# Retention attention into a gated MLP on one core: q and k in one tile, early values scaled on GpSimd, conversions and loads half a period earlier

## The chip, the core and the metric

The kernel runs on one core of a Trainium2 chip. The core has five engines that work side by side, each with its own queue of instructions that it takes in order: TensorE (PE) multiplies matrices, VectorE (DVE) and ScalarE (ACT) do elementwise work, GpSimd (POOL) does elementwise work and issues DMAs, and SyncE (SP) issues DMAs. The metric is the time of one execution on the device in microseconds (us), as the median of several runs. Smaller is better.

## What is computed

The first part is a recurrent attention (retention) with a decay for each head; the second is an MLP whose activation is h times cos(h). There are 4 batch elements, 8 heads, 768 positions and a head size of 64; the MLP has 3072 tokens, a model width of 512 and an inner width of 2048. All inputs and the output are float32.

```python
gamma = 1.0 - 2.0 ** (-5.0 - np.arange(H))
for t in range(S):
    state = gamma * state + outer(k[:, :, t], v[:, :, t])
    y[:, :, t] = (1 / sqrt(D)) * (q[:, :, t] @ state)
x = y.transpose(0, 2, 1, 3).reshape(B * S, H * D)
h = x @ w_in
out = (h * cos(h)) @ w_out
```

## The kernel before

**Chunks and pairs.** The sequence is cut into six chunks of 128 positions. One step of the attention handles one chunk of two batch elements, called a pair `p`; there are twelve pairs, six for batch elements 0 and 1 and then six for 2 and 3. The index `b` in 0, 1 names the batch element within a pair. The decay is separated into a factor on q that shrinks with the position (`gq`) and a factor on v that grows with it (`gk`); then the product of q and k within a chunk needs only a mask of zeros and ones, and the state that passes from chunk to chunk needs no decay.

**The steps of one pair.** `load` (line 110) brings float32 tiles of q, k and v (256 KB each) into SBUF. `conv_q`, `conv_k` and `conv_v` (lines 169 to 184) turn them into bfloat16: q times `gq` into `qs`, k copied into `ks`, v times `gk` into `vs`. There are three buffers of each, used in turn. The transposes of q and k into `qkt` are made by TensorE for pairs 0 to 3 (`stage_t`, line 191: eight transposes into one PSUM bank, then one copy of the bank by DVE or ACT) and by two DMA transposes on SP for pairs 4 to 11 (`stage_t_dma`, line 204: one for all of q, one for all of k). `stage_a` (line 217) multiplies k by q into two PSUM banks, `stage_m` (line 231) multiplies these by the mask into `am` on DVE, and `stage_y` (line 238) multiplies `am` by the values, adds the part that comes from the state `stb`, copies the result into `xt` on ACT, and updates the state in PSUM (`st_ps`), which it then copies into `stb`.

**The MLP.** A group `g` is two pairs, thus 512 tokens. `unit_f` (line 283) and `pair_f` (line 291, for the tokens of one pair) multiply `xt` by a part of `w_in`; `act` (line 274) makes the cosine on ACT and the product on DVE into `gt`. `unit_o` (line 307) multiplies `gt` by `w_out`, copies the bank on ACT, and stores it from SP.

**The order.** It is written out by hand (lines 341 to 480): each engine gets its instructions in the order in which the program lists them, and waits only where data or a buffer requires it. PSUM banks are taken from a list and given back to its end (class `Banks`). `warm(n)` (line 332) puts n matmuls of zeros into TensorE's queue. At the start pair 0 is handled separately: q is only cast, the decay and the mask are multiplied in as one factor `decay` that ACT makes with eight exponentials, and the values are cast without decay into `vu`; `conv_v(0)` on GpSimd is only for the state. GpSimd's queue at the start is: five loads of pairs 0 and 1 and more, `w_in` part 0, `conv_v(0)`, `w_in` part 1, `conv_v(1)`, `w_in` parts 2 and 3, the parts of `w_out` and the loads of pairs 2 and 3. In the steady part, `ahead(p + 1)` (line 435) converts a pair at the start of the half period before its use, `stage_t_dma(p + 1)` follows one unit later, and `later(p)` (line 441) does `stage_y(p)` and loads pair p + 3.

Of the kernel before, what the change touches and what calls it, by code (L numbers as in the profile page):

```python
# [10 lines left out]
FP32 = mybir.dt.float32  # L11
BF16 = mybir.dt.bfloat16
# [18 lines left out]
def kernel(  # L31
# [9 lines left out]
    nc = tc.nc  # L41
# [22 lines left out]
    def sb(shape, dt, name):  # L64
        return const.tile(shape, dt, name=name)
# [20 lines left out]
    qs = [sb([128, 2, H, D], BF16, f"qs{i}") for i in range(NB)]  # L86
    ks = [sb([128, 2, H, D], BF16, f"ks{i}") for i in range(NB)]
# [13 lines left out]
    rel = sb([128, 2, 128], FP32, "rel")  # L101
    decay = sb([128, H, 128], FP32, "decay")
    vu = sb([128, 2, H, D], BF16, "vu")
# [25 lines left out]
    def w_in_t(i, f):  # L129
# [6 lines left out]
    nc.gpsimd.iota(rel[:, 0], pattern=[[1, 128]], base=0, channel_multiplier=-1,  # L136
                   allow_small_or_imprecise_dtypes=True)
    nc.gpsimd.iota(pos, pattern=[[C, NC]], base=1, channel_multiplier=1,
                   allow_small_or_imprecise_dtypes=True)
    load(nc.gpsimd, 0, ("v0", "v1"))  # L140
    load(nc.gpsimd, 1, ("k0", "k1", "q1", "v0", "v1"))
# [3 lines left out]
    for h in range(H):  # L145
        nc.vector.memset(lgv[:, h : h + 1], lg[h])
    nc.vector.tensor_scalar(out=ident, in0=rel[:, 0], scalar1=0.0, scalar2=None,
                            op0=ALU.is_equal)
    nc.vector.tensor_scalar(out=rel[:, 1], in0=rel[:, 0], scalar1=0.0, scalar2=1.0e6,
                            op0=ALU.is_lt, op1=ALU.mult)  # L150
    nc.vector.tensor_tensor(out=rel[:, 1], in0=rel[:, 1], in1=rel[:, 0], op=ALU.add)
    nc.vector.tensor_scalar(out=mask, in0=rel[:, 0], scalar1=0.0, scalar2=None,
                            op0=ALU.is_ge)
    for h in range(H):
        nc.scalar.activation(out=decay[:, h], in_=rel[:, 1], func=AF.Exp, bias=lnsc,
                             scale=float(lg[h]))
    nc.vector.tensor_tensor(out=lgp, in0=pos.unsqueeze(2).to_broadcast([128, NC, H]),
                            in1=lgv.unsqueeze(1).to_broadcast([128, NC, H]), op=ALU.mult)
    nc.scalar.activation(out=gq, in_=lgp, func=AF.Exp, bias=lnsc)
    nc.scalar.activation(out=gk, in_=lgp, func=AF.Exp, scale=-1.0)  # L160
    nc.scalar.activation(out=cosb[0][:, :8], in_=lgp[:, 0, :], func=AF.Sin, scale=0.0)
    for t in stb:
        nc.vector.memset(t, 0.0)


    def bc(g, c):
        return g[:, c, :].unsqueeze(2).to_broadcast([128, H, D])

    def conv_q(p, eng):
        for b in range(2):  # L170
            eng.tensor_tensor(out=qs[p % NB][:, b], in0=qf[SLOT[p]][b],  # L171
                              in1=bc(gq, p % NC), op=ALU.mult)

    def conv_v(p, eng):
        for b in range(2):
            eng.tensor_tensor(out=vs[p % NB][:, b], in0=vf[SLOT[p]][b],  # L176
                              in1=bc(gk, p % NC), op=ALU.mult)

    def conv_k(p, on_act):
        for b in range(2):  # L180
            if on_act:
                nc.scalar.copy(out=ks[p % NB][:, b], in_=kf[SLOT[p]][b])  # L182
            else:
                nc.vector.tensor_copy(out=ks[p % NB][:, b], in_=kf[SLOT[p]][b])
# [6 lines left out]
    def stage_t(p, b, on_act):  # L191
        n = p % NB
        bank = banks.take()
        tr = bank.bitcast(BF16).rearrange("p (w a t) -> p w a t", w=2, a=HP)
        for w, src in enumerate((qs[n], ks[n])):
            for a in range(HP):
                nc.tensor.transpose(tr[:, w, a, :], src[:, b, 2 * a : 2 * a + 2, :], ident)  # L197
        if on_act:
            nc.scalar.copy(out=qkt[n][:, :, b], in_=tr)
        else:  # L200
            copy_bits(qkt[n][:, :, b], tr)
        banks.give(bank)

    def stage_t_dma(p):
        n = p % NB
        for w, src in enumerate((qs[n], ks[n])):
            nc.sync.dma_start_transpose(
                out=qkt[n][:, w].rearrange("p b a t -> p (b a) t"),
                in_=src.rearrange("p b h d -> p (b h d)"))

    def qt(n, b, a):
        return qkt[n][:, 0, b, a, :]

    def kt(n, b, a):
        return qkt[n][:, 1, b, a, :]
# [13 lines left out]
    decay_j = decay.rearrange("p (a j) t -> p j a t", j=2)  # L229

    def stage_m(p, item, parts=(0, 1)):
        b, bk, ap = item
        for j in parts:
            by = decay_j[:, j] if p == 0 else mask.unsqueeze(1).to_broadcast([128, HP, 128])
            nc.vector.tensor_tensor(out=am[p % 2][b][j], in0=ap[j], in1=by, op=ALU.mult)  # L235
            banks.give(bk[j])

    def stage_y(p, copy_st=nc.vector.tensor_copy):
        c = p % NC
        n = p % NB  # L240
        for b in range(2):
            bank = banks.take()
            yp = bank.rearrange("p (a t) -> p a t", a=HP)
            for a in range(HP):
                if c > 0:
                    for j in range(2):
                        nc.tensor.matmul(  # L247
                            yp[ts(j, 64), a, :], lhsT=stb[p % 2][:, b, a, ts(j, 64)],
                            rhs=qt(n, b, a), start=True, stop=False,
                            skip_group_check=True)  # L250
                for j in range(2):
                    nc.tensor.matmul(  # L252
                        yp[ts(j, 64), a, :], lhsT=(vu if p == 0 else vs[n])[:, b, 2 * a + j, :],
                        rhs=am[p % 2][b][j][:, a, :], start=(c == 0), stop=True,
                        skip_group_check=True)
            nc.scalar.copy(out=xt[(p // 2) % 2][:, :, ts(2 * (p % 2) + b, C)], in_=yp)  # L256
            banks.give(bank)
        if c == NC - 1:
            return
        for b in range(2):  # L260
            for a in range(HP):
                for j in range(2):
                    h = 2 * a + j
                    nc.tensor.matmul(  # L264
                        st_ps[ts(j, 64), b, a, :], lhsT=ks[n][:, b, h, :],
                        rhs=vs[n][:, b, h, :], start=(c == 0 and b == 0 and a == 0),
                        stop=True, skip_group_check=True)
        for j in range(2):
            copy_st(out=stb[(p + 1) % 2][ts(j, 64), :, :, ts(j, 64)], in_=st_ps[ts(j, 64)])  # L269

# [69 lines left out]

    load_w_in(0)
    conv_v(0, nc.gpsimd)
    load_w_in(1)
    conv_v(1, nc.gpsimd)
    load_w_in(2)
    load_w_in(3)
# [6 lines left out]

    warm(10)
    nc.vector.tensor_copy(out=qs[0][:, 0], in_=qf[0][0])
    for b in range(2):
        nc.vector.tensor_copy(out=ks[0][:, b], in_=kf[0][b])
    stage_t(0, 0, False)
    nc.vector.tensor_copy(out=qs[0][:, 1], in_=qf[0][1])  # L359
    for b in range(2):  # L360
        nc.scalar.copy(out=vu[:, b], in_=vf[0][b])
    a00 = stage_a(0, 0)
    stage_m(0, a00, (0,))
    stage_t(0, 1, False)
    stage_m(0, a00, (1,))
    warm(1)
    stage_m(0, stage_a(0, 1))
    conv_k(1, True)
    conv_q(1, nc.vector)
    warm(2)  # L370
    stage_y(0, nc.scalar.copy)
    stage_t(1, 0, False)
    stage_t(1, 1, True)
    warm(2)
    attend(1)
    banks.give(spare)
    pair_f(0, 0, (0,))
    stage_y(1, nc.scalar.copy)
    pair_f(0, 0, (1,))
    pair_f(1, 0)  # L380
# [5 lines left out]
    for part in range(3):  # L386
        for j in range(4):
            unit_o(0, j, part)
            if part == 2 and j == 0:
                stage_t(2, 0, False)  # L390
                stage_t(2, 1, False)
                conv_v(2, nc.vector)
            elif part == 2 and j == 1:
                stage_m(2, stage_a(2, 0))
            elif part == 2 and j == 3:
                stage_m(2, stage_a(2, 1))
# [12 lines left out]
    stage_t(3, 0, False)  # L409
    stage_t(3, 1, False)  # L410
# [16 lines left out]
    stage_t_dma(5)  # L427
    pair_f(3, 1)
# [3 lines left out]
    conv_v(6, nc.gpsimd)  # L432
    pair_f(3, 3)

    def ahead(p):
        if p < NP:
            conv_q(p, nc.gpsimd)
            conv_k(p, True)
            conv_v(p, nc.gpsimd)

    def later(p):
        stage_y(p)
        if p + 3 < NP:
            load(nc.sync, p + 3, ("q0", "q1", "v0"))
            load(nc.gpsimd, p + 3, ("k0", "k1", "v1"))
# [6 lines left out]
    stage_t_dma(6)  # L452
# [6 lines left out]
    for g in range(2, NG + 1):  # L459
        for s in range(16):  # L460
# [8 lines left out]
            if p < NP:  # L469
                if r == 0:  # L470
                    ahead(p + 1)
                elif r == 1:
                    todo = [stage_a(p, b) for b in range(2)]
                    stage_m(p, todo[0])
                    if p + 1 < NP:
                        stage_t_dma(p + 1)
                elif r == 2:
                    stage_m(p, todo[1])
                elif r == 5:
                    later(p)  # L480
# [30 lines left out]
```

## Time and profile before

| what | value |
|---|---|
| median of 7 runs (lowest to highest) | 211.75 us (211.05 to 215.66) |
| the profiled execution: time, span of its instructions | 213.54 us, 211.8 us |
| mean granted TensorE clock | 0.981 |
| DVE conversion of q, lines 171: shortest, longest in the first 60 us | 681 ns, 2877 ns |
| GpSimd conversion of v, line 176, mean | 1048 ns |
| ACT copy of k, line 182, mean | 614 ns |
| mask on DVE, line 235, mean | 681 ns |
| issue of one load by GpSimd, line 115 | about 0.9 us |
| share of 16 DMA engines: SP's queue, GpSimd's queue | 37.0%, 29.6% |

The page gives busy time by engine, then 40 equal slices of the span, in which each digit is the busy share in tenths; the row PEclk is the TensorE clock that was granted. The chain of waits follows the end of the execution back from instruction to instruction: each row is a start, a duration and a name. A row of the timeline is a start, a duration, the engine, the line of the kernel, the operation, its output and inputs, and how many instructions were merged. A row of the stretches table has the stretch, its length, then for each engine (PE, its weight loads, DVE, ACT, POOL) the busy time and number of instructions, then the granted clock, the mean share of the DMA engines, and GB/s.

### The profile page before, as it was taken

What the parts mean: (1) busy time and instruction counts of PE and PEld (TensorE: products, weight loads), DVE (VectorE), ACT (ScalarE), POOL (GpSimd) and SP (SyncE); (2) the same over time, 40 slices, a digit from 0 to 9 for tenths busy, and PEclk for the clock granted to TensorE, in tenths of its full rate; (3) what the DMA queues carried; (4) which work ended last, traced back from release to release, by engine and by line L of the source; (5) the groups of instructions that cost most, each with busy time, mean ns of one, the idle gap of its engine ahead of it and who ended that gap; (6) DMA issues with size and microseconds to landing.
All of it is one profiled execution on the core that took longest, in us unless ns stands there. A gap on an engine that the chain in (4) does not pass through costs nothing.

```text
span 211.8 us, 4149 instructions
## 1 busy us (share of the span) xinstructions
PE 202.3 (96%) x1631; PEld 112.8 (53%) x1631; DVE 116.7 (55%) x192; ACT 114.9 (54%) x190; POOL 86.5 (41%) x99
## 2 busy tenths in 40 slices
PE   7569999999999999999999999999999999999992
PEld 2346754547999555555555445445445444444440
DVE  4796587090976764949674474474473333343000
ACT  5754886218799435666745745744545554553110
POOL 7998238499967907999261500000000000000000
PEclk9886999999999999999999999999999999999998
DMA  6999999999999999999999231231101101110121
GB/s 152 339 245 203 216 260 290 336 249 341 265 154 262 180 307 246 230 279 150 261 231 223 79 83 51 71 81 50 50 3 50 50 0 53 50 51 26 74 96 56
DMA packets 54884, 33.83 MB, mean 160 GB/s; under 512 B 46224, under 2 KB 48528, under 8 KB 54864
## 3 DMA queue, kind: packets, MB, share of 16 engines
q1 hardware_dynamic: 48432, 17.44, 37.0%
q0 software_dynamic: 6288, 15.99, 29.6%
q8 instruction: 13, 0.21, 0.4%
q10 hardware_dynamic: 144, 0.13, 0.2%
q14 instruction: 7, 0.06, 0.1%
HBM read 27.26 MB, written 6.29 MB: 158 GB/s over the span
## 4 chain that ended last, share of the span: by engine, by line
PE 90%; DVE 5%; DMA 2%; issue 1%; ACT 1%; SPq 0%; DVEq 0%; ACTq 0%
PE bank L312 39%; PE bank L286 31%; PE bank L298 8%; PE bank L224 3%; PE bank L247 3%; PE bank L252 2%; DMA kf<-in_k_dram 2%; DVE qkt L187 2%; DVE qs L171 2%; PE st_ps L264 1%; PE bank L197 1%; PE bank L334 0%; DVE qs L359 0%; DVE am L235 0%; ACT cosb L277 0%
## 5 line engine op out<-in xcount | busy, mean ns | idle before, releaser
L281 DVE TENSOR_TENSOR gt<-bank,cosb 128x512 bf16<-128x512 f32 x96 | 65.5, 689 | 63.6 <-ACT cosb L277 63.2
L277 ACT ACTIVATE cosb<-bank,halfpi 128x512 bf16<-128x512 f32 x96 | 65.4, 687 | 53.0 <-PE bank L286 46.8
L312 PE MATMUL bank<-w_out_sb,gt 128*128 128x512 bf16 x384 | 93.3, 379 | 0.0
L286 PE MATMUL bank<-xt,w_in 128*128 128x512 bf16 x304 | 75.1, 380 | 0.0
L312 PEld LDWEIGHTS <-gt 128*128 128x128 bf16 x384 | 36.7, 98 | 42.8
L286 PEld LDWEIGHTS <-w_in 128*128 128x128 bf16 x304 | 33.8, 114 | 30.8 <-issue 0.2
L235 DVE TENSOR_TENSOR am<-bank,mask 128x512 bf16<-128x512 f32 x44 | 27.8, 681 | 1.8 <-PE bank L224 1.8
L171 POOL TENSOR_TENSOR qs<-qf,gq 128x512 bf16<-128x512 f32 x18 | 18.5, 1048 | 22.0 <-DMA qf<-in_q_dram 18.8
L324 ACT COPY ob<-bank 128x512 f32<-128x512 f32 x23 | 13.4, 587 | 24.1 <-PE bank L312 24.0
L176 POOL TENSOR_TENSOR vs<-vf,gk 128x512 bf16<-128x512 f32 x22 | 22.5, 1048 | 1.0 <-DMA vf<-in_v_dram 1.0
L115 POOL DMA_DIRECT2D kf<-in_k_dram x23 | 21.0, 914 | 2.0 <-DMA w_out_sb<-in_moe_w_out_dram 1.2
L298 PE MATMUL bank<-xt,w_in 128*128 128x256 bf16 x160 | 19.3, 279 | 0.0
L298 PEld LDWEIGHTS <-w_in 128*128 128x128 bf16 x160 | 17.4, 115 | 1.0 <-issue 0.2
L115 POOL DMA_DIRECT2D vf<-in_v_dram x17 | 15.1, 887 | 4.9 <-DMA w_out_sb<-in_moe_w_out_dram 4.9
L182 ACT CAST ks<-kf 128x512 bf16<-128x512 f32 x22 | 12.6, 614 | 4.9 <-DMA kf<-in_k_dram 4.8
L256 ACT CAST xt<-bank 128x512 bf16<-128x512 f32 x24 | 12.9, 588 | 3.7 <-DVE gt L281 3.0
L247 PEld LDWEIGHTS <-stb 128*64 128x64 bf16 x160 | 8.7, 110 | 3.9 <-issue 3.4
L252 PE MATMUL bank<-am,vs 128*64 128x128 bf16 x176 | 10.7, 219 | 0.0
L247 PE MATMUL bank<-qkt,stb 128*64 128x128 bf16 x160 | 10.3, 222 | 0.0
L269 DVE CAST stb<-st_ps 64x512 bf16<-64x512 f32 x12 | 8.2, 687 | 3.5 <-PE st_ps L264 3.3
L224 PE MATMUL bank<-qkt 64*128 64x128 bf16 x192 | 8.4, 229 | 1.3 <-DVE qkt L187 1.1
L252 PEld LDWEIGHTS <-vs 128*64 128x64 bf16 x176 | 9.4, 110 | 0.4 <-issue 0.4
(48 smaller groups left out, 77.7 us busy)
## 6 DMA issues: line engine op xcount, KB each, us to landing
kf<-in_k_dram POOLq DMA_DIRECT2D x23, 256.0 KB, 5.6
out_dram<-ob SPq DMA_DIRECT2D x23, 256.0 KB, 2.1
qf<-in_q_dram SPq DMA_DIRECT2D x19, 256.0 KB, 6.4
vf<-in_v_dram POOLq DMA_DIRECT2D x17, 256.0 KB, 5.9
w_in<-in_moe_w_in_dram POOLq DMA_DIRECT2D x4, 512.0 KB, 6.6
w_out_sb<-in_moe_w_out_dram POOLq DMA_DIRECT2D x4, 512.0 KB, 12.4
vf<-in_v_dram SPq DMA_DIRECT2D x7, 256.0 KB, 5.4
qf<-in_q_dram POOLq DMA_DIRECT2D x5, 256.0 KB, 7.3
```

Of the source, the lines that this page charges most:

```text
L115: eng.dma_start(out=t[SLOT[p]][b], in_=src[2 * bp + b, :, ds(c * C, C)].rearrange("h t d -> t h d"))
L171: eng.tensor_tensor(out=qs[p % NB][:, b], in0=qf[SLOT[p]][b], in1=bc(gq, p % NC), op=ALU.mult)
L176: eng.tensor_tensor(out=vs[p % NB][:, b], in0=vf[SLOT[p]][b], in1=bc(gk, p % NC), op=ALU.mult)
L224: nc.tensor.matmul(ap[j][:, a, :], lhsT=kt(n, b, a)[po : po + 64, :], rhs=qt(n, b, a)[po : po + 64, :], tile_position=(po, 0))
L235: nc.vector.tensor_tensor(out=am[p % 2][b][j], in0=ap[j], in1=by, op=ALU.mult)
L247: nc.tensor.matmul(yp[ts(j, 64), a, :], lhsT=stb[p % 2][:, b, a, ts(j, 64)], rhs=qt(n, b, a), start=True, stop=False, skip_group_check=True)
L252: nc.tensor.matmul(yp[ts(j, 64), a, :], lhsT=(vu if p == 0 else vs[n])[:, b, 2 * a + j, :], rhs=am[p % 2][b][j][:, a, :], start=(c == 0), ...
L277: nc.scalar.activation(out=cb, in_=bank, func=AF.Sin, bias=halfpi)
L281: nc.vector.tensor_tensor(out=out, in0=bank, in1=cb, op=ALU.mult)
L286: nc.tensor.matmul(bank, lhsT=w_in_t(i, f), rhs=xt[g % 2][:, i, :], start=(i == 0), stop=(i == KIN - 1))
L298: nc.tensor.matmul(bank[:, ts(e, 256)], lhsT=w_in_t(i, f + e), rhs=xt[g % 2][:, i, ts(hf, 256)], start=(i == 0 and e == 0), stop=(i == KIN ...
L312: nc.tensor.matmul(bank, lhsT=gt[g % 2][:, f, ts(j, 128)], rhs=w_out_sb[:, f, :], start=(f == 0), stop=(f == KOUT - 1))
```

## The change

**Tiles.** `qs` and `ks` become one tile `qk` of three buffers, laid out by batch element b, then q or k. `qkt` is laid out likewise. `stage_t_dma` still issues two DMA transposes for a pair, now one for each b that holds q and k of it; before it was one for q and one for k. `stage_t` copies always on DVE, and can put fillers between the transposes of q and those of k.

**Start.** Pair 0 is now treated as the others: q times `gq`, the mask of zeros and ones, v times `gk` in `vs`. The tiles `decay` and `vu`, the eight exponentials and two DVE operations on `rel` are gone. k of pair 0 is cast on ACT, before on DVE. `stage_y` is split into `half_y` for one b, and `stage_s` for the state. In GpSimd's queue the conversions of v of pair 0 stand between loads, v of pair 1 is loaded after the first of them, and `conv_v(1)` uses `gk2`, a copy of a part of `gk` that DVE makes after `conv_q(1)`. The fillers are laid out differently.

**Steady part.** `ahead` is gone; `later(p)` now converts pair p + 2 and issues its DMA transposes, and then loads pair p + 4. Loads of pair 7 and the transposes of pair 6 move forward in the same way.

```diff
     load(nc.gpsimd, 0, ("k1",))
-    nc.gpsimd.iota(rel[:, 0], ...)
     nc.gpsimd.iota(pos, ...)
+    nc.gpsimd.iota(rel, ...)
     load(nc.gpsimd, 0, ("v0", "v1"))
-    load(nc.gpsimd, 1, ("k0", "k1", "q1", "v0", "v1"))
+    load(nc.gpsimd, 1, ("q1", "k0", "k1"))
...
-    for h in range(H):
-        nc.scalar.activation(out=decay[:, h], in_=rel[:, 1], func=AF.Exp, bias=lnsc,
-                             scale=float(lg[h]))
+    for t in stb:
+        nc.vector.memset(t, 0.0)
     nc.vector.tensor_tensor(out=lgp, ...)
+    nc.vector.tensor_scalar(out=ident, in0=rel, ...)
+    nc.vector.tensor_scalar(out=mask, in0=rel, ...)
...
     def stage_t_dma(p):
         n = p % NB
-        for w, src in enumerate((qs[n], ks[n])):
+        for b in range(2):
             nc.sync.dma_start_transpose(
-                out=qkt[n][:, w].rearrange("p b a t -> p (b a) t"),
-                in_=src.rearrange("p b h d -> p (b h d)"))
+                out=qkt[n][:, b].rearrange("p w a t -> p (w a) t"),
+                in_=qk[n][:, b].rearrange("p w h d -> p (w h d)"))
...
+    conv_v(0, nc.gpsimd, (0,))
+    load(nc.gpsimd, 1, ("v0", "v1"))
     load_w_in(0)
-    conv_v(0, nc.gpsimd)
+    conv_v(0, nc.gpsimd, (1,))
     load_w_in(1)
-    conv_v(1, nc.gpsimd)
     load_w_in(2)
+
+    warm(8)
+    conv_q(0, nc.vector)
+    conv_k(0, True)
+    stage_t(0, 0, 3)
+    warm(2)
+    stage_t(0, 1)
+    a00 = stage_a(0, 0)
+    stage_m(0, a00)
+    stage_m(0, stage_a(0, 1))
+    conv_k(1, True)
+    conv_q(1, nc.vector)
+    nc.vector.tensor_copy(out=gk2, in_=gk[:, :2])
+    conv_v(1, nc.gpsimd, g=gk2)
     load_w_in(3)
...
-    warm(10)
-    nc.vector.tensor_copy(out=qs[0][:, 0], in_=qf[0][0])
...
-    stage_y(0, nc.scalar.copy)
-    stage_t(1, 0, False)
-    stage_t(1, 1, True)
-    warm(2)
-    attend(1)
+    warm(2)
+    half_y(0, 0)
+    warm(2)
+    half_y(0, 1)
     warm(1)
+    stage_t(1, 0)
+    stage_t(1, 1)
+    warm(1)
+    stage_s(0, nc.scalar.copy)
+    a10 = stage_a(1, 0)
+    stage_m(1, a10)
+    warm(1)
+    stage_m(1, stage_a(1, 1))
+    warm(1)
     banks.give(spare)
     pair_f(0, 0, (0,))
-    stage_y(1, nc.scalar.copy)
+    half_y(1, 0)
     pair_f(0, 0, (1,))
+    half_y(1, 1)
+    stage_s(1, nc.scalar.copy)
     pair_f(1, 0)
...
     stage_t_dma(5)
+    load(nc.sync, 7, ("q0", "q1", "v0"))
+    load(nc.gpsimd, 7, ("k0", "k1", "v1"))
     pair_f(3, 1)
     pair_f(3, 2)
     conv_q(6, nc.gpsimd)
     conv_k(6, True)
     conv_v(6, nc.gpsimd)
+    stage_t_dma(6)
     pair_f(3, 3)
...
     def later(p):
         stage_y(p)
-        if p + 3 < NP:
-            load(nc.sync, p + 3, ("q0", "q1", "v0"))
-            load(nc.gpsimd, p + 3, ("k0", "k1", "v1"))
+        n = p + 2
+        if 6 < n < NP:
+            conv_q(n, nc.gpsimd)
+            conv_k(n, True)
+            conv_v(n, nc.gpsimd)
+            stage_t_dma(n)
+        if p + 4 < NP:
+            load(nc.sync, p + 4, ("q0", "q1", "v0"))
+            load(nc.gpsimd, p + 4, ("k0", "k1", "v1"))
...
-    stage_t_dma(6)
...
-                if r == 0:
-                    ahead(p + 1)
-                elif r == 1:
+                if r == 1:
                     todo = [stage_a(p, b) for b in range(2)]
                     stage_m(p, todo[0])
-                    if p + 1 < NP:
-                        stage_t_dma(p + 1)
```

## The prediction

> **What bounds the kernel now.** I read the page first: busy shares, then the slices.
>
> ```profile
> PE 202.3 (96%) x1631; PEld 112.8 (53%) x1631; DVE 116.7 (55%) x192; ACT 114.9 (54%) x190; POOL 86.5 (41%) x99
> ...
> PE   7569999999999999999999999999999999999992
> ...
> PEclk9886999999999999999999999999999999999998
> ```
>
> TensorE is full except in the first four slices (21 us) and the last. The waits view names only 5.4 us of PE waits, all before 16 us. From about 21 us on, the chain is matmuls; the change removes none of them, and the tail after 208 us is untouched. So a gain must come from the start: the question is when `pair_f(1,0)`, from which PE runs without a gap, begins. The chain of waits, from 5.5 us:
>
> ```profile
> 11.94 3.42 DVE qs L171 x2
> 15.36 0.04 issue
> 15.40 0.63 PE bank L197 x8
> 16.04 0.85 PE bank L334 x2
> 16.89 0.97 PE bank L224 x16
> 17.86 1.70 PE bank L298 x8
> ...
> 20.82 2.74 PE bank L298 x24
> ```
>
> The first line is pair 1's q conversion on VectorE: 3.42 us for two instructions. The last line is 24 matmuls at 0.114 us; eight belong to `pair_f(0,0,(1,))`, so `pair_f(1,0)` begins at 20.82 + 0.91 = **21.7**. Why the conversion is slow is in GpSimd's timeline:
>
> ```profile
> 9.91 2.08 POOL L176 TENSOR_TENSOR vs<-vf,gk 128x512 bf16<-128x512 f32 x2
> 11.90 0.82 POOL L120 DMA_DIRECT2D w_in<-in_moe_w_in_dram  x1
> 12.74 2.05 POOL L176 TENSOR_TENSOR vs<-vf,gk 128x512 bf16<-128x512 f32 x2
> 14.73 1.55 POOL L120 DMA_DIRECT2D w_in<-in_moe_w_in_dram  x2
> ```
>
> The q tile's view gives 693 ns for the first conversion (11.85) and 2877 for the second (12.47): it ends 0.56 us after GpSimd's two v conversions end at 14.79. The first overlapped a DMA issue and lost nothing. The table of stretches, cut where the clock record steps (the number before the last two is the granted clock):
>
> ```profile
> 5.64:9.05 3.41, 1.55 (x26) 1.03 (x23) 2.78 (x5) 2.68 (x6) 3.41 (x4) 1.00 1.16 344
> 9.05:12.47 3.42, 3.06 (x34) 1.47 (x33) 3.18 (x6) 2.13 (x4) 3.42 (x5) 0.50 1.03 328
> 12.47:15.88 3.41, 1.39 (x35) 1.18 (x32) 3.41 (x3) 1.85 (x4) 3.39 (x5) 1.00 1.24 207
> 15.88:19.29 3.41, 3.41 (x29) 1.90 (x26) 1.90 (x5) 1.01 (x1) 3.41 (x6) 0.50 1.23 203
> ```
>
> A stretch with PE busy 41 to 45% is followed by one at half clock, one with 90% or more by full clock.
>
> **What the skill says.** "SBUF — State Buffer", section "SBUF: two separate sides": a VectorE operation with two SBUF inputs and a GpSimd operation that reads SBUF exclude each other for a whole instruction, and the one that starts first goes first. The trace agrees on exclusion (2877 against 693 ns), less on order: VectorE's record starts 0.27 us earlier, and it lost. "TensorE: Matmul & The Clock Gate", section "What's actually happening": the clock follows PE activity in free-running windows of 3413 ns; the record steps by just that. "DMA: Bandwidth & Descriptors", section "Issuing engines are not separate DMA queues": all queues share 16 DMA engines. The trace agrees: their share is 1.03 to 1.24 in the four rows above.
>
> **The change, part by part.** Times are from issue plus landing time in each tile's view.
>
> *Start of pair 0.* Removed: 8 exponentials on ACT (8 x 0.39, overlapping, 2.45 us), two rel operations, four DVE casts, two vu casts. This saves nothing by itself, since pair 0 waits for its loads: q0 lands 3.8, k0 6.1, q1 7.0, v0 7.7, v1 9.1. GpSimd's orders up to v1 are unchanged. gq now follows lgp directly: iotas end 2.8, lgp and gq (0.21 + 0.32) 3.4, in time for q0; the Sin table (1.28) is in by 5; the two stb memsets (1.03) fill DVE's old wait for rel (1.40). k goes to ACT: 6.1 + 0.62 = 6.75 against DVE's 6.59. conv_q b1 is 7.0 to 7.7 and stands ahead of the first qkt copy on DVE: copies 7.7 and 8.45, then four masks at 0.6 us spacing (their starts at 17.46 to 19.27 are 0.6 apart), ended by 11.6; before 11.94.
>
> *v on GpSimd.* vs b0: v0's landing 7.75 + 1.06 = 8.8. Pair 1's v loads move behind it (two at 0.88: 10.6), then w_in 0 (0.78: 11.4), vs b1 (12.45), w_in 1 and 2 (14.0). Pair 1's q1 now goes ahead of k0 and k1, which land one load later (0.76 us: 10.8, 11.6; needed about 13). Masks read PSUM: beside GpSimd's conversions at 9.9 to 12.0 they took 680 to 691 ns, so these cost DVE nothing. conv_q(1) b0 at 11.6 does meet vs b1: it runs after 12.45, and b1 ends at **13.7** (2 x 0.62). gk2 is a DVE copy of 16 numbers: between 0.06 (smallest memset) and 0.21 us (lgp); I take 0.1. It keeps GpSimd's conv_v(1) off until q is done: 15.35 becomes 13.7, **1.65 us earlier**. Behind that wait on GpSimd stand conv_v(1) (13.9 to 16.0, needed about 17), w_in 3 and fourteen loads; DMA still has w_in 1 and 2 (2.5 us each, spacing of landings) to move until about 20.8, so these lose nothing.
>
> *To the stream.* Pair 1 needs two copies, now both on DVE (1.3; ACT's of 1.01 goes), state matmuls, transposes, masks: copies 13.8 to 15.0, stage_a 14.7 to 15.1, four masks 15.2 to 17.7. w_in 0 is issued 1.46 us later than before, but its own 6.4 us from issue had queueing in it: DMA moves all earlier loads by 13.1 and 2.5 more lands it at 15.6 if the queue never runs dry, 10.6 + 6.4 = 17.0 if it needs as long; I take 16.0. Then `pair_f` 16.0 to 16.9 (8 x 0.114), half_y 0.46 (two took 0.92), `pair_f` to 18.3, half_y to 18.8. A new wait appears: pair_f(1,0) needs the xt copy of that half_y directly, and on ACT the copy stands behind a cosine (0.69): 18.5 + 0.69 + 0.6 = 19.85. Before, a `pair_f` covered it. At full clock the gain is 21.7 - 19.85 = 1.85 us.
>
> *Clock.* Six more fillers (21 for 15; 0.43 us each at half clock) lie in waits. If 12.47 to 15.88 is at half clock, half_y, filler, eight transposes and stage_s put the masks at 16.5 to 18.9 and pair_f(1,0) at 21.0: gain 0.7. PE there follows a stretch busy some 45 to 60%, by these sums; the trace doesn't show which side that is. Bounds 0.7 and 1.85; the phase differs between runs, so I take 1.2, near the middle.
>
> *Shared q/k tiles, half a period ahead.* Still two transposes per pair on SP, each of 1024 columns, so no copying saved. But both halves of pair 4 now wait for conv_k(4) on ACT (56.0); before, q's went at 53.0. Queued behind them on SP are loads 6 and transposes 5, and pair 7's loads (three on GpSimd at 61.7, before 68.8; three on SP ahead of transposes 6). From pair 7 on, conversions start half a period earlier, which only adds slack; ACT's two casts (2 x 0.61) fit its idle time. What is next late is pair 5:
>
> ```profile
> 63.85 1.67 SPq L207 DMA_TRANSPOSE qkt<-qs  x1
> 65.61 1.26 SPq L207 DMA_TRANSPOSE qkt<-ks  x1
> ```
>
> The second lands 4.5 us after issue, 70.1; PE reads it at 73.4, with the gain at 72.2. Three GpSimd loads beside it add 3 x 0.76 (spacing of landings at the start) = 2.3: 72.4. I take a cost of 0 to 0.2 and count 0.1 into the rounding. The lower bound is 0, for transposes are already two per pair; the upper is a rival below.
>
> **Sum.** Gain 1.2: the profiled execution, 213.54 (span 211.8 and 1.7 around it), would be 212.3. Its own time stands 1.8 above the median of the seven runs, so the forecast is 211.75 - 1.2 = **210.6** (0.5% and a little).
>
> **Rivals.** (1) *Warm start*: fillers keep the clock full, and w_in 0 lands at 15.6: gain 1.85 to 2.3, **209.7**. For it: more fillers; against: the chain has the same waits for loads. (2) *The gain is given back at attend(5)*: PE waits there until its former time: **211.8**. For it: the slack of 3.3 us is spent by 1.2 + 2.3; against: DMA share was only 0.61 in 62 to 64. (3) *Slower*: pair 5's transposes land as late as those at 93 to 95 us did beside GpSimd loads, 8.6 to 9.6 us after issue against 3.8 to 4.5. Issued at 65.6 that is 75.1, so PE is 1.7 behind its time of before: **213.5**. It decides once landing passes 73.4; against: at 93 SP and GpSimd both had loads outstanding. (4) *Nothing gained at the start*: two half-clock stretches or w_in 0 at 17.0 put pair_f(1,0) at 21.0 to 22: **211.5**.
>
> **Numbers.** Chances: forecast 0.42, (1) 0.13, (2) 0.17, (3) 0.18, (4) 0.10. A difference under about 0.5% (1.06 us) can't be told from no change here. Forecast's spread (bounds 0.7 and 1.85) puts three quarters of its chance beyond 0.5%: faster 0.32 + 0.13 = 0.45; same 0.10 + 0.17 + 0.08 = 0.35; slower 0.20 (rival 3 and 0.02 of 4). Range 209.4 to 213.0: from the top of (1) into (3), leaving out under 0.2. The likeliest case alone spans 209.9 to 211.1.
>
> **What would show it.** Right: DVE's two conv_q(1) end by 13.9; GpSimd's conv_v(1) begins after them; pair_f(1,0) begins between 19.5 and 21.0, with an ACT copy as its releaser; no PE wait after. Wrong: a PE wait on qkt at 60 to 82 us (rivals 2, 3), half clock after 15.9, conv_q(0) b1 caught by vs b0 at 7.7, or stream steps longer than before.

## The result, and the profile after

The changed kernel takes **220.56 us** (median of 12 runs, 213.92 to 222.49) against 211.54 for the kernel before (31 runs, 210.63 to 215.66). Nine of the twelve runs lie over 1.5% above the fastest and count as slow, so the ratio is taken from the other three (213.92, 215.25 and 215.51) and is 1.0153 (95% interval 1.011 to 1.0196); the profile below is of one of the nine (221.27 us, span 219.5), and none of the three was profiled. The change is slower by either measure, and the forecast was 210.6 with a range to 213.0. Below, a bracket behind a ratio is its 95% interval.

The page of the changed kernel, busy shares and slices:

```profile
PE 205.3 (94%) x1637; PEld 113.5 (52%) x1637; DVE 115.5 (53%) x190; ACT 111.3 (51%) x181; POOL 86.9 (40%) x99
...
PE   7765999999999994999999999999999999999992
...
PEclk9997999999999999799999999999999999999999
```

The engines' work is nearly what it was. New are a PE slice of 4 (near 85 us), a clock slice of 7 right behind it, and a fourth slice (16.5 to 22 us) of 5, where before it was 9. The waits view of PE names what it waited for (total, times, longest):

```profile
PE bank L215 <- DMA qkt<-qk: 3.4, 3, 1.8
PE bank L296 <- DMA w_in<-in_moe_w_in_dram: 2.4, 1, 2.4
```

Neither row is in the view of before. A third new row, 1.8 us for GpSimd's `vs`, ends at 13.05; PE comes to the wait for `w_in` 0 early all the same, so it costs nothing at the stream. The row for `w_in` is at the start, in PE's timeline:

```profile
18.92 1.52 PE L296 MATMUL bank<-xt,w_in 128*128 128x256 bf16 x8 [2.35 <-DMA w_in<-in_moe_w_in_dram]
...
21.38 1.72 PE L296 MATMUL bank<-xt,w_in 128*128 128x256 bf16 x8
...
24.35 0.81 PE L296 MATMUL bank<-xt,w_in 128*128 128x256 bf16 x6 [0.43 <-ACT xt L245]
```

These are `pair_f(0,0,(0,))`, `pair_f(0,0,(1,))` and `pair_f(1,0)`. The first waits 2.35 us for w_in 0; eight matmuls then take 1.52 and 1.72 us where they take 1.06 at full clock, because the idle stretch is followed by half clock (19.38 to 22.79). `pair_f(1,0)` begins at 24.35, before at 21.7. VectorE ended when it was forecast to:

```profile
11.42 2.13 DVE L163 TENSOR_TENSOR qk<-qf,gq 128x512 bf16<-128x512 f32 x2
13.47 0.26 DVE L357 COPY gk<-gk 128x16 f32<-128x16 f32 x1
```

The q conversion of pair 1 ends at 13.55, the copy that holds GpSimd off it follows, and GpSimd's `conv_v(1)` begins at 14.51. That gain is real; w_in 0, which landed at 18.88, is later than all it freed. Where w_in 0 stands is in GpSimd's timeline:

```profile
7.92 1.04 POOL L168 TENSOR_TENSOR vs<-vf,gk 128x512 bf16<-128x512 f32 x1 [0.80 <-DMA vf<-in_v_dram]
8.91 1.81 POOL L113 DMA_DIRECT2D vf<-in_v_dram  x2
10.71 0.78 POOL L118 DMA_DIRECT2D w_in<-in_moe_w_in_dram  x1
```

GpSimd waits 0.8 us for v0 of pair 0 and converts it; pair 1's v loads (8.91, 9.84) and w_in 0 (10.71) are queued behind that. Before, they were issued at 7.39, 8.27 and 9.14.

The other three waits are at 76.9 (0.50, pair 5), 85.6 (1.04) and 87.8 (1.81, both pair 6). SP's own timeline shows why:

```profile
59.26 5.49 SPq L198 DMA_TRANSPOSE qkt<-qk  x2
64.80 2.92 SPq L113 DMA_DIRECT2D qf<-in_q_dram  x2
67.82 1.47 SPq L113 DMA_DIRECT2D vf<-in_v_dram  x1
69.47 5.69 SPq L198 DMA_TRANSPOSE qkt<-qk  x2
75.22 1.22 SPq L113 DMA_DIRECT2D qf<-in_q_dram  x2
76.54 1.00 SPq L113 DMA_DIRECT2D vf<-in_v_dram  x1
77.72 4.20 SPq L198 DMA_TRANSPOSE qkt<-qk  x2
```

Pairs 4, 5 and 6 in turn, with the loads of pairs 6 and 7 between. Before, pair 5's transposes were issued at 63.85 and 65.61 and pair 6's at 67.04 and 68.36, with no load between them; now pair 6's come at 77.72 and 80.23, behind the loads of pair 7, and land at 85.54 and 87.76. The table of stretches of the same kernel shows the price of such waits beyond the wait itself (PE's busy time first; the granted clock is the number before the last two):

```profile
84.10:87.60 3.50, 0.85 (x11) 0.23 (x8) 2.65 (x4) 1.05 (x2) 2.96 (x4) 1.00 1.09 203
87.60:91.00 3.40, 3.20 (x15) 1.36 (x16) 0.00 (x0) 0.00 (x0) 1.16 (x2) 0.51 1.20 345
```

PE is busy for 0.85 of 3.5 us, and the next 3.4 us run at half clock: 1.7 us of full-speed work more. **The difference of the two spans, 219.5 - 211.8 = 7.7**, is then accounted for: 24.35 - 21.7 = 2.65 at the start, 3.4 in the qkt waits, 1.7 in the half-clock stretch. The granted clock of this execution, 0.984, is the two stretches named and nothing else: 6.8 us at half clock are 3.4 of 219.5. The sum is that of the execution shown; how the 3 to 4 us of the three shortest runs split is not shown.

### The profile page after: what moved, and what is told of

It reads as the page before. It is cut to its first block, busy times and chain, and to the rows that moved or that the text cites. A ratio compares the mean times of both kernels' runs of the same rounds, so it can differ in the third digit from the quotient of the medians.

```text
span 219.5 us, 4163 instructions
## 1 busy us (share of the span) xinstructions
PE 205.3 (94%) x1637; PEld 113.5 (52%) x1637; DVE 115.5 (53%) x190; ACT 111.3 (51%) x181; POOL 86.9 (40%) x99
## 4 chain that ended last, share of the span: by engine, by line
PE 58%; DMA 21%; POOL 15%; issue 3%; SPq 1%; DVE 0%; ACT 0%; POOLq 0%; DVEq 0%
PE bank L310 29%; PE bank L284 25%; DMA qf<-in_q_dram 8%; DMA w_out_sb<-in_moe_w_out_dram 7%; POOL vs L168 4%; DMA qkt<-qk 3%; POOL kf L113 3%; POOL qk L163 3%; DMA vf<-in_v_dram 2%; POOL vf L113 2%; PE bank L215 2%; POOL w_in L118 1%; PE bank L236 1%; PE bank L241 1%; SPq L198 1%
## 5 line engine op out<-in xcount | busy, mean ns | idle before, releaser
L223 DVE TENSOR_TENSOR am<-bank,mask 128x512 bf16<-128x512 f32 x48 | 30.3, 681 | 0.2
L168 POOL TENSOR_TENSOR vs<-vf,gk 128x512 bf16<-128x512 f32 x22 | 23.0, 1067 | 12.3 <-PE st_ps L257 5.7
L163 POOL TENSOR_TENSOR qk<-qf,gq 128x512 bf16<-128x512 f32 x18 | 18.6, 1046 | 14.2 <-DMA qf<-in_q_dram 12.6
L296 PE MATMUL bank<-xt,w_in 128*128 128x256 bf16 x160 | 19.8, 283 | 2.8 <-DMA w_in<-in_moe_w_in_dram 2.4
L174 ACT CAST qk<-kf 128x512 bf16<-128x512 f32 x24 | 13.9, 623 | 9.3 <-DMA kf<-in_k_dram 9.3
L241 PE MATMUL bank<-am,vs 128*64 128x128 bf16 x192 | 12.4, 224 | 1.8 <-POOL vs L168 1.8
L241 PEld LDWEIGHTS <-vs 128*64 128x64 bf16 x192 | 10.3, 112 | 3.3 <-POOL vs L168 2.3
L236 PE MATMUL bank<-qkt,stb 128*64 128x128 bf16 x160 | 10.9, 227 | 0.0
```

The lines of the kernel that those rows point to most:

```text
L163: eng.tensor_tensor(out=qk[p % NB][:, b, 0], in0=qf[SLOT[p]][b], in1=bc(gq, p % NC), op=ALU.mult)
L174: nc.scalar.copy(out=qk[p % NB][:, b, 1], in_=kf[SLOT[p]][b])
L236: nc.tensor.matmul(yp[ts(j, 64), a, :], lhsT=stb[p % 2][:, b, a, ts(j, 64)], rhs=qt(n, b, a), start=True, stop=False, skip_group_check=True)
L241: nc.tensor.matmul(yp[ts(j, 64), a, :], lhsT=vs[n][:, b, 2 * a + j, :], rhs=am[p % 2][b][j][:, a, :], start=(c == 0), stop=True, skip_grou ...
L296: nc.tensor.matmul(bank[:, ts(e, 256)], lhsT=w_in_t(i, f + e), rhs=xt[g % 2][:, i, ts(hf, 256)], start=(i == 0 and e == 0), stop=(i == KIN ...
```

## The experiments

The **theory**: two losses in two places. (a) At the start, pair 1's v loads and w_in 0 stand behind `conv_v(0)` in GpSimd's queue, and w_in 0 lands late. (b) In the steady part, loads placed ahead of a pair's transposes make these late. **Rivals**: one loss, of which the other is only a consequence; or the shared q/k tile, since a transpose of one b has to wait for both conversions. In each profile I read two numbers: when `pair_f(1,0)` begins ("stream start"), and the rest of the span from there.

**Two halves of the change, and the tile alone.** e1 has the changed kernel's start and tiles, and from `stage_t_dma(5)` on the text of before, with `ahead`, the loads of pair p + 3, and `stage_t_dma(6)` after `attend(4)`:

```diff
     stage_t_dma(5)
-    load(nc.sync, 7, ("q0", "q1", "v0"))
-    load(nc.gpsimd, 7, ("k0", "k1", "v1"))
...
-    stage_t_dma(6)
...
+    stage_t_dma(6)
```

> New start and shared tiles, but conversions, loads and transposes from pair 5 on in the old order. Theory A (two separate losses: w_in 0 lands late at the start, and from pair 5 on the transposes stand behind more on SP's queue): keeps the loss of the start alone, pair_f(1,0) near 24 us, at most 0.5 us of PE waits on qkt, 213.5 to 214.5 us. Theory B (one loss: the late start alone pushes everything behind it): 218 to 221 as the changed kernel, with the waits on qkt still there.

Measured: 214.63 (4 runs, 213.73 to 218.13), 1.014 [1.0083, 1.0197]. w_in 0 is issued at 11.79 and lands at 20.02; the stream starts at 26.45, the rest is 189.9. Its waits view:

```profile
PE bank L296 <- DMA w_in<-in_moe_w_in_dram: 2.8, 1, 2.8
```

and no row for qkt. The start loses by itself. (The profile is of the longest of the four runs, 218.13; half clock from 19.17 to 26.0 is in its start.)

e2 is the other half: the start of before, the shared tile, and from `stage_t_dma(5)` on the changed text.

> Old start, shared tiles, conversions and loads half a period ahead. Theory A: pair_f(1,0) at 21.7 as before, but PE waits 2 to 4 us on qkt of pairs 5 and 6, and a stretch of half clock may follow: 214 to 217 us. Theory B: no waits on qkt, 211.5 us.

Measured: 214.56 (4, 213.09 to 218.03), 1.0128 [1.0054, 1.0202]. w_in 0 lands at 15.93, stream start 20.29, rest 190.8, one qkt wait of 0.34 in the profile. The order of the steady part loses by itself too, and the theory of one loss falls. Its one profile shows only a part of the ratio: 0.7 more rest than before's 190.1; half clock from 8.18 to 15.01, which the order of the steady part can't have caused, is in its start.

e3 is the kernel before with the shared tile alone:

```diff
-        for w, src in enumerate((qs[n], ks[n])):
+        for b in range(2):
             nc.sync.dma_start_transpose(
-                out=qkt[n][:, w].rearrange("p b a t -> p (b a) t"),
-                in_=src.rearrange("p b h d -> p (b h d)"))
+                out=qkt[n][:, b].rearrange("p w a t -> p (w a) t"),
+                in_=qk[n][:, b].rearrange("p w h d -> p (w h d)"))
```

> The kernel before with q and k of a batch element in one tile and one DMA transpose, all else as it was. Theory A, if the order of loads does it: pair 4's transposes go out 3 us later but no PE wait follows, 211.5 to 212. Theory C (the shared tile itself does it, since both transposes wait for ACT's copy of k and then run together): waits on qkt of 1 us and more, 213 and above.

Measured: 211.72 (20, 210.84 to 215.48), 1.0011 [0.9984, 1.0037]: nothing that can be told from no change. Its profile has one qkt wait, 1.8 us at 93.3, with the order of before: a wait in one execution is no verdict on an edit, the ratio is. e3 also shows the start of before in another execution, in PE's timeline:

```profile
15.93 1.06 PE L297 MATMUL bank<-xt,w_in 128*128 128x256 bf16 x8 [0.16 <-DMA w_in<-in_moe_w_in_dram]
...
18.19 2.81 PE L297 MATMUL bank<-xt,w_in 128*128 128x256 bf16 x24
```

With 16 of the last row's 24 matmuls left after `pair_f(0,0,(1,))`, the stream starts at 19.1, not at 21.7, and what released its first matmul is already w_in.

e4 is the changed kernel with one transpose for q and one for k, as before:

```diff
-        for b in range(2):
+        for w in range(2):
             nc.sync.dma_start_transpose(
-                out=qkt[n][:, b].rearrange("p w a t -> p (w a) t"),
-                in_=qk[n][:, b].rearrange("p w h d -> p (w h d)"))
+                out=qkt[n][:, w].rearrange("p b a t -> p (b a) t"),
+                in_=qk[n][:, w].rearrange("p b h d -> p (b h d)"))
```

> The changed kernel with one transpose for q of both batch elements and one for k, as before the change. Theory A: pair 4's q goes out ahead, but pair 7's loads still stand ahead of pair 6's transposes: 217 to 221, waits on qkt remain. Theory C: the waits on qkt go, leaving the loss of the start: 213.5 to 214.5.

Measured: 217.14 (4, 215.1 to 219.55), 1.0241 [1.0163, 1.0319], stream start 23.81, w_in 0 at 19.88, rest 191.0, a qkt wait of 0.71 at 84.4. Its profile is of a run of 216.56, so the late `w_in` 0 is not confined to the longest executions. Both losses stay, and e3 has the tile without either: the tile is not what causes them. Whether it adds to the second is open, since e4's rest is less than the changed kernel's 195.1 and its four runs lie within the spread of that kernel's.

**Loss (a): w_in 0 first.** e5 is the changed kernel with this edit alone:

```diff
-    load(nc.gpsimd, 1, ("q1", "k0", "k1"))
+    load(nc.gpsimd, 1, ("q1", "k0", "k1", "v0", "v1"))
...
-    conv_v(0, nc.gpsimd, (0,))
-    load(nc.gpsimd, 1, ("v0", "v1"))
     load_w_in(0)
-    conv_v(0, nc.gpsimd, (1,))
+    conv_v(0, nc.gpsimd)
```

> The changed kernel with GpSimd's queue at the start as it was up to w_in 0: pair 1's v loads and w_in 0 stand ahead of pair 0's v conversions. Theory A (the v conversion between loads lets GpSimd's DMA queue run dry, and w_in 0 lands 3 to 4 us late): w_in 0 lands near 16, pair_f(1,0) at 19.5 to 20.5, what is left is the loss of the new order, 213 to 217. Theory D (w_in 0 is late because GpSimd converts right behind it, wherever it stands): w_in 0 still takes 8 us from its issue, lands at 17 or later, gain under 1 us.

Measured: 213.06 (4, 212.91 to 216.27), 1.0073 [1.0043, 1.0103]. w_in 0 is issued at 8.87 and lands at 15.44, stream start 19.37. The late start is cured by the place of these loads alone. The rest is 191.7, 1.8 over that of e6 below, and waits for qkt remain:

```profile
PE bank L215 <- DMA qkt<-qk: 1.5, 2, 1.0
```

e6 has that start and the steady part of before (the edits of e5 and e1 together).

> New start with w_in 0 and pair 1's v loads ahead as in e5, and the old order from pair 5 on: both suspected losses taken out, shared tiles and gk2 kept. Theory A: pair_f(1,0) at 19.2 to 19.8, 211 to 212 us, as the kernel before, since w_in 0 at 16 us bounds both. Theory D: 213 and above. If the masks and the q conversion bounded the start of before, 210 or less.

Measured: 212.01 (4, 211.13 to 213.26), 1.003 [0.9977, 1.0084], no qkt wait, rest 189.9. Its stream start:

```profile
15.56 1.07 PE L296 MATMUL bank<-xt,w_in 128*128 128x256 bf16 x8
...
19.44 1.91 PE L296 MATMUL bank<-xt,w_in 128*128 128x256 bf16 x16 [0.43 <-ACT xt L245]
```

So with both losses undone the kernel is back at the time of before: all that is left of the change (masks, v on GpSimd, the earlier q conversion, the split `stage_y`) brings nothing measurable as a whole. w_in 0 lands at 15.5 as it did before, and the split adds a wait of 0.43; e10 takes that out.

The mirror of e5 is e9: the kernel before with only the changed order of GpSimd's first queue.

```diff
-    load(nc.gpsimd, 1, ("k0", "k1", "q1", "v0", "v1"))
+    load(nc.gpsimd, 1, ("k0", "k1", "q1"))
...
+    conv_v(0, nc.gpsimd, (0,))
+    load(nc.gpsimd, 1, ("v0", "v1"))
     load_w_in(0)
-    conv_v(0, nc.gpsimd)
+    conv_v(0, nc.gpsimd, (1,))
```

> The kernel before with only GpSimd's queue at the start as in the change: vs b0 of pair 0 stands in front of pair 1's v loads and of w_in 0, vs b1 behind w_in 0. Nothing else is changed. Theory A (this alone makes w_in 0 late): w_in 0 lands at 18.5 to 20 instead of 15.6 to 16, its slowest sixteenth a microsecond or more behind the others, and PE waits for it: 213.5 to 215. Theory E (the rest of the new start, the q conversion or the split of stage_y, costs the time): w_in 0 at 17 at most, 211.5 to 212.5.

Measured: 215.83 (4, 215.01 to 216.65), 1.0195 [1.0147, 1.0244], stream start 23.13 against 18.8 to 20.3 in the kernels with the start of before, rest 190.1. The order alone costs about 4 us. But my expectation missed the route: w_in 0 did land late, at 17.98, and PE never waited for it. In e9 the conversion of q of pair 1 still meets GpSimd's of v, and all that is later on GpSimd makes it later (2.95 us for the first of the two instructions, 0.68 for the second):

```profile
12.72 3.56 DVE L171 TENSOR_TENSOR qs<-qf,gq 128x512 bf16<-128x512 f32 x2
```

It ends at 16.28, in before at 15.36, and the clock is half from 8.46 to 18.70, so the transposes and `stage_a` behind it run until 19.08. All four runs have a clock of 0.976 to 0.984, so this is not one execution's accident. In e9's profile the order cost through this chain; in the changed kernel, e1, e4 and e12, where that conversion is out of the way, through w_in 0.

**Loss (b): which part of "half a period ahead".** e7 is e2 with pair 7's loads put behind the transposes of pair 6:

```diff
     stage_t_dma(5)
-    load(nc.sync, 7, ("q0", "q1", "v0"))
-    load(nc.gpsimd, 7, ("k0", "k1", "v1"))
...
     stage_t_dma(6)
+    load(nc.sync, 7, ("q0", "q1", "v0"))
+    load(nc.gpsimd, 7, ("k0", "k1", "v1"))
```

> e2 (old start, new order) with pair 7's loads put behind pair 6's transposes on SP and behind pair 6's conversions on GpSimd. If these six loads are what makes pair 6 late: 211.5 to 212.5, no PE wait on qkt of pairs 5 and 6. If the conversions and transposes that are half a period ahead do it: 213.5 to 215.5, as e2.

Measured: 212.04 (4, 210.83 to 216.31), 1.0008 [0.9964, 1.0052]. SP in e7:

```profile
62.81 7.27 SPq L206 DMA_TRANSPOSE qkt<-qk  x4
70.13 2.29 SPq L114 DMA_DIRECT2D qf<-in_q_dram  x2
```

Pairs 5 and 6 are transposed in one run from 62.81, and pair 6's land at 70.4 and 73.5; PE reads them at 78.65. No wait on pairs 5 or 6 is left (one of 0.7, on pair 7). The place of two lines of loads is all of loss (b) that can be measured with the old start; e7 moves SP's and GpSimd's together, so which of them counts is not separated.

e8 is e2 with the conversions and transposes of pairs 7 to 11 back in their old places, only the loads staying early (pair p + 4):

```diff
     def later(p):
...
-        n = p + 2
-        if 6 < n < NP:
-            conv_q(n, nc.gpsimd)
-            conv_k(n, True)
-            conv_v(n, nc.gpsimd)
-            stage_t_dma(n)
...
+                if r == 0 and p + 1 < NP:
+                    conv_q(p + 1, nc.gpsimd)
+                    conv_k(p + 1, True)
+                    conv_v(p + 1, nc.gpsimd)
...
+                    if p + 1 < NP:
+                        stage_t_dma(p + 1)
```

> e2 with conversions and transposes of pairs 7 to 11 back at their old place, so that only loads (pair p + 4 for p + 3) and pair 6's transposes are ahead. If loads 7 do it: 213.5 to 215.5, as e2. If the conversions ahead do it: 211.5 to 212.5.

Measured: 223.12 (4, 219.74 to 226.83), 1.0413 [1.0366, 1.046]: far beyond what I expected on either side.

```profile
PE bank L223 <- DMA qkt<-qk: 9.7, 5, 2.8
```

Five waits, between 72.6 and 103.1, and half clock at 84.4 and again from 101.5 to 108.3. Beside e3, e8 has only the loads and pair 6's transposes ahead, so these hurt, and by e7 most likely the loads; beside e2 it lacks the conversions and transposes ahead, so these are what makes the loads bearable.

**A better version.** e6's last wait is for the `xt` copy on ACT, which the prediction had named. e10 is e6 with a `pair_f` over it again, as in before:

```diff
-    half_y(1, 0)
+    stage_y(1, nc.scalar.copy)
     pair_f(0, 0, (1,))
-    half_y(1, 1)
-    stage_s(1, nc.scalar.copy)
     pair_f(1, 0)
```

> e6 with stage_y(1) in one piece and pair_f(0,0,(1,)) behind it, as in the kernel before, so that the xt copy of the second half lies beside eight matmuls. If the wait for that copy (0.43 us in e6) and the split cost what they seem to: pair_f(1,0) at 18.7 to 19.0, 0.4 to 0.7 us under e6, 210.6 to 211.3. If w_in 0 alone bounds: as e6, 211.5.

Measured: **210.74** (14, 210.5 to 211.81), 0.9946 [0.9923, 0.997]: faster than both kernels.

```profile
15.71 1.06 PE L296 MATMUL bank<-xt,w_in 128*128 128x256 bf16 x8 [0.27 <-DMA w_in<-in_moe_w_in_dram]
...
17.97 2.81 PE L296 MATMUL bank<-xt,w_in 128*128 128x256 bf16 x24
```

The wait on ACT is gone, the stream starts at 17.97 + 0.91 = 18.9, 0.56 before e6's. Its runs also spread less (1.3 us over 14 runs; before 2.8 over 23 beside it). Most of the gain lies there: the best runs are 210.5 and 210.86, but the granted clock is 0.996 or more in all 14 runs and under 0.996 in 16 of the 23 of before. The gain has the size that the forecast gave the start, 1.2 us; whether the fillers or the earlier conversion keep the clock up was not separated.

e11 puts w_in 0 ahead of pair 1's v loads in e10:

```diff
+    load_w_in(0)
     load(nc.gpsimd, 1, ("v0", "v1"))
-    load_w_in(0)
```

> e10 with w_in 0 issued ahead of pair 1's two v loads. If w_in 0 bounds the start: it lands at 14.0 to 14.5, and pair_f(0,0,(0,)) begins near 15.1 where masks and stage_a leave off; pair 1's v lands 1.5 us later and conv_v(1) ends near 17, so pair_f(1,0) at 18.5 to 18.9: 210.3 to 211. If the late v then bounds: as e10 or up to 0.5 us above.

Measured: 210.74 (11, 210.55 to 212.08), 0.9954 [0.993, 0.9977]. w_in 0 lands at 14.51, a microsecond before PE asks for it at 15.48, and the time is that of e10. The second case of the expectation came: pair 1's v now lands at 15.3 and 16.0, and PE waits 0.36 us at 17.51 for GpSimd's conversion of it, so the stream starts at 18.27 + 0.91 = 19.2, 0.3 after e10's. In e10 and e11 PE reaches `pair_f(0,0,(0,))` at about 15.5; w_in 0 costs time there only when it is later.

e12 is the changed kernel once more, unchanged, for its spread.

> The changed kernel once more, for a second profile. Theory A: w_in 0 lands at 18.5 to 20 again and pair_f(1,0) begins at 23 to 26, against 19 to 20 in the kernels with the old queue; waits on qkt between 70 and 90 us of 0.5 us and more; 214 to 221.

Measured: 220.7 (4, 213.9 to 222.32), without a ratio. w_in 0 at 19.52, stream start 23.45, rest 195.4. Its waits view:

```profile
PE bank L215 <- DMA qkt<-qk: 3.8, 2, 2.0
PE bank L296 <- DMA w_in<-in_moe_w_in_dram: 2.7, 1, 2.7
```

The qkt waits lie on pair 5 this time (76.9 and 79.3), and half clock follows from 79.2 to 82.6. Pair 5's transposes have no load of pair 7 ahead of them on SP here; GpSimd issues pair 7's loads beside them:

```profile
66.58 4.86 SPq L198 DMA_TRANSPOSE qkt<-qk  x2
```

```profile
66.32 1.80 POOL L113 DMA_DIRECT2D kf<-in_k_dram  x2
```

The two are issued at 66.58 and 68.30 and land at 76.9 and 79.3, 10.3 and 11.0 us later. In e5, where GpSimd's loads of pair 7 are beside them too, it is 7.9 and 7.7; in e6 and e7, where they follow from about 68 us, 4.2 to 5.8. So by these profiles the loads make transposes late in two ways, ahead of them on SP (pair 6 in the first profile) and beside them (pair 5 here). Against a usual execution of before (stream start 19.3, the mean of e2, e3, e7 and e8, and rest 190.0, as in before's profile, e1 and e6) e12 loses 4.2 at the start and 5.4 after: 9.6, where its median is 8.7 over that of before beside it.

## Why the prediction was wrong, step by step

**Right.** The q conversion ends at 13.55 (forecast 13.7) and the copy keeps GpSimd off it. The end was hit by another order than forecast, and so in part by luck: the first of the two instructions ran at once (0.68 us), and the second (1.53) ran beside GpSimd's `vs` b1 (11.49 to 12.99) and ended 0.55 after it. w_in 0 was issued at 10.71 (forecast 10.6). As rival 1 had it, the new start keeps the clock up: it stayed full until 19.4, and through the whole start in e5, e6, e10, e11 and e12 (not in e4, half from 13.6 to 17.0), while the start of before met half clock in five of six profiles (not in e7). Whether the fillers do it was not separated. The new wait on ACT's `xt` copy is there, 0.43 us. Three of the marks named for the start hold (conversion, its order with GpSimd's, ACT as releaser); the stream start between 19.5 and 21.0 and "no PE wait after" fail, and two signs of being wrong came, a PE wait on qkt at 76.9 and half clock after 15.9.

**Wrong: "w_in 0 at 16.0", in the step "To the stream".** The bounds were 15.6 ("if the queue never runs dry") and 17.0 (issue plus 6.4, which "had queueing in it"). It took 8.2 from issue, 18.88. Both bounds took a load 1.5 us later in the queue to land at most 1.5 us later. It landed 3.3 later. A load counts as landed when the last of 16 parts is in: 14 of w_in 0's were in by 16.9, within the bounds, and the last two came at 18.6 and 18.9. So of the 2.9 us over the forecast's 16.0, 0.9 are a slower transfer and 2.0 are the last two parts, a term that the sum doesn't have. The table of stretches shows the slower transfer, in the changed kernel

```profile
12.00:14.00 2.00, 0.95 (x16) 0.74 (x17) 1.73 (x3) 1.39 (x3) 2.00 (x3) 1.00 0.89 174
14.00:16.00 2.00, 2.00 (x45) 1.36 (x43) 1.66 (x3) 0.76 (x3) 2.00 (x3) 1.00 1.11 161
16.00:18.00 2.00, 0.57 (x9) 0.17 (x5) 2.00 (x4) 0.49 (x1) 2.00 (x4) 1.00 0.99 150
```

and in e6, where the same loads were issued 1.5 us or more earlier:

```profile
12.00:14.00 2.00, 2.00 (x40) 1.37 (x35) 2.00 (x5) 1.14 (x3) 1.92 (x3) 1.00 1.18 219
14.00:16.00 2.00, 1.62 (x29) 1.10 (x25) 1.78 (x4) 1.16 (x2) 2.00 (x3) 1.00 1.24 205
16.00:18.00 2.00, 2.00 (x30) 1.64 (x28) 1.54 (x3) 1.16 (x2) 2.00 (x5) 1.00 1.25 208
```

The last number is GB/s. From 12 to 18 us the changed kernel moves 162 on average and e6 211: the queue did run thin, and stayed slow while w_in 0 was on its way. No rival had w_in 0 later than 17.0, and the worst put the stream at 22. In the sum this term is 18.9 in place of 16.0, with half clock on top.

**Wrong: the base of the gain, 21.7.** The forecast took 1.2 us off the profiled execution and then off the median, though the profiled execution stood 1.8 above that median and the text says so. That 1.8 was at the start: of four other kernels with the start of before, the stream begins at 18.8 in e7 (no half-clock stretch), 19.1 and 19.3 in e3 and e8 (one) and 20.3 in e2 (two, like before's 21.7). In these w_in 0, at 15.6 to 16.0, is level with the chain through q, and PE waits 0.2 to 0.6 for it in three of them; in such an execution there is little for a faster q conversion to gain. e6 shows none (1.003), e10 0.5%. A gain at the start that is read from one execution has to be measured from the usual one.

**Wrong in size and place: "half a period ahead, a cost of 0 to 0.2".** Rival 3 had the mechanism, transposes that land late beside GpSimd's loads, with 1.7 us on pair 5. What came was 3.4 of waits, most of them on pair 6, or 3.8 on pair 5 (e12), and then 1.7 at half clock, which the rival left out. e12 is that rival as it stands, 10.3 and 11.0 us from issue to landing in place of its 8.6 to 9.6. The forecast added 2.3 us for three loads to a landing of 4.5. And it names pair 7's loads "ahead of transposes 6" but prices pair 5 alone; in the first profile they push back pair 6, whose transposes stand behind them on SP: issued from 77.72 in place of 67.04, 10.7 us later, of which the later start is 2.65. There is a third part to it: SP's two issues for pair 4 and for pair 5 took 5.49 and 5.69 us, where before a single one for pairs 4 to 6 took 1.2 to 2.1.

**What stays open.** In medians over all runs the start alone costs 1.6% (e1), the order alone 1.6% (e2) and both 4.3%; in the ratios it is 1.4, 1.3 and 1.5%. So most executions of the changed kernel lose more than the two parts and a few lose less, and why was not tested. Why w_in 0 was late is settled as to its cause (the place of the loads, e5 and e9), not as to why the transfer stays slower than in e6 until about 17 us or why the last parts lag.

## What to carry to other kernels

A step moved into a DMA-issuing queue is to be priced by the loads behind it: ask whether the queue still has work outstanding at that moment, and if it may run dry, don't take the delay of the issue for the delay of the landing (1.6 us of issue became 3.3 us of landing here). Put loads for a later pair behind the transposes of the nearer one, on SP and on GpSimd alike. And before forecasting a gain at a place, see in more than one execution that the place is as slow as the profile says.

## What the runs showed of the hardware that was not expected

- **A few shares lag.** A load's completion comes in 16 parts. In before, those of w_in 0 all land within 14.7 to 15.6. In the changed kernel 14 land from 15.7 to 16.9 and the last two at 18.6 and 18.9; in e12 15 by 17.3 and the last at 19.5; in e4 15 by 17.7 and the last at 19.9; in e9 14 by 16.7 and the last two at 17.4 and 18.0. With the v loads back in front (e6) all are within 14.8 to 15.5. PE waits for the last. Why one or two lag wasn't tried.
- **Issue time of a DMA transpose isn't fixed.** On SP a single one took 1.23 to 3.91 us in before (the longest at 95.03) and up to 4.28 in the changed kernel (69.47 to 73.75), with all of SP's queue behind it.
- **A wait costs more than itself.** 2.85 us of waits at 85 to 88 us were followed by 3.4 us at half clock, 1.7 more. But not every wait: in e12 the 2.75 us before 19.57, which fell across two stretches, were followed by full clock.
- **How busy is busy enough for full clock.** The clock record steps by 3.41 us. All fourteen profiles were divided at its steps, from the first step to 205 us. Stretches at full clock in which PE was busy for 43% or less were all followed by half clock (nine; 0.72 us of 3.41 in the changed kernel at 84.23, 1.47 in e2 at 4.77), those with 56% or more all by full clock (1.90 in e11 at 6.13). Between 44 and 52% it went either way (1.63 in e12 at 17.79: full; 1.75 in e8 at 5.88: half). The prediction's open case, 45 to 60%, lies across this border.
